# Transposes moved into freed score banks, copies ahead of norms, a split last block, and idle matmuls in TensorE's waits

## The chip, the cores and the metric

One core of a Trainium2 chip. The metric is the device time of one execution in microseconds (us), lower is better. Every run is set against runs of the kernel before on the same chip in the same rounds. A ratio is the mean time of one kernel's fast runs over the mean of the other's fast runs of the same rounds, so it is not quite the ratio of the medians that stand beside it; its interval is a 95% one.

## The reference, cut to what matters

Sliding-window attention with ALiBi, then a dense hard-swish feed-forward layer over all tokens.

```python
# q, k, v: (8 batches, 8 heads, 576, 64)
rel = pos[:, None] - pos[None, :]
mask = (rel >= 0) & (rel < 128)
scores = where(mask, q @ k.T / 8 - slope[h] * abs(rel), -1e9)
attn = softmax(scores) @ v
x = attn as (4608 tokens, 512)
h = x @ w_in                         # 512 -> 2048
out = (h * clip(h + 3, 0, 6) / 6) @ w_out    # 2048 -> 512
```

## The kernel before: the parts that matter

The kernel works in 32 steps `g`, four pairs of heads for each of eight batches. In a step TensorE makes scores in two two-bank PSUM tiles, ScalarE exponentiates them, GpSimd masks them, TensorE multiplies by v (`values`), VectorE normalises, and the result is transposed into `xT`. `fill` puts matmuls of the feed-forward layer between these parts. Batches 0 to 2 transpose q and k on TensorE (`transposes`); from batch 3 on a DMA transpose reads them out of `tbuf`, where GpSimd casts them. The pools with `PSUM` in them hold the banks that TensorE's results go to.

Names in the views: `pr` is the copy that feeds the transposes, `tp` their result, `qTb` and `kTb` the copies out of it; `scd` and `sco` are scores, `pd`, `po` and `p4buf` their exponentials, `vbuf` is v after its cast, `av` and `avh` come out of `values`, `avs` is normalised; `hps` is an up-projection, `r` and `g` what ScalarE and VectorE make of it, `ops` the down-projection. PE is TensorE, DVE VectorE, ACT ScalarE, POOL GpSimd, SP SyncE. A line of a timeline has start, length, engine, line of the kernel, operation, and in brackets how long the engine idled before and what ended that.

```python
ps_sc = tile_pool(bufs=2, space=PSUM)   # two tiles of two banks: scores
ps_h  = tile_pool(bufs=2, space=PSUM)   # two tiles of one bank: hps, tp, ...

def transposes(g):
    b, hp = divmod(g, NP)               # NP = 4
    for nm, dst in (("q", qTb[b % 2]), ("k", kTb[b % 2])):
        src = st.pop((g, nm))...
        tp = ps_h.tile([128, RT, RP], BF16, tag="h", name="tp", ...)
        for t in range(RT):             # RT = 6
            nc.tensor.transpose(tp[:, t, :], src[:, t, :], ident[:RP, :RP])
        eng = nc.scalar.copy if nm == "k" and (g == 0 or g > 2 * NP) else nc.vector.tensor_copy
        eng(out=dst..., in_=tp...)

def segment(lo, hi, fills):             # steps 5 and later
    for g in range(lo, hi + 1):
        # ... (cut)
        scores(g)
        if pe_next:
            transposes(g + 1)
        fill(f[0]); exp_diag(g, 0); fill(f[1]); exp_diag(g, 1)
        values(g - 1, (0, 1, 2))
        fill(f[2]); exp_off(g, 0); fill(f[3]); exp_off(g, 1)
        values(g - 1, (3, 4))
        # ... fill, back(g - 1), prepare(g + 2), fill, stage_next(g), fill

def stage_next(g):                      # loads, casts, DMA transposes to come
    # ... (cut)
    if g == 8:
        cast_tokens(3, "q")             # GpSimd, five casts into tbuf
    if g == 9:
        load_tokens(3, "v")
        xbar(3, "q")                    # DMA transpose out of tbuf
        cast_tokens(3, "k")             # waits for it: tbuf is one buffer
    if g == 10:
        xbar(3, "k")
    # ... (cut; batches 4 to 7 alike)
```

The softmax here doesn't subtract the row's maximum and nothing guards it: scores larger than these inputs give would overflow.

## Time and profile before

| | before |
|---|---|
| time, median of 4 fast runs | 343.48 us (342.02 to 343.56) |
| the profiled run, and its span | 340.97 us, 339.24 us |
| TensorE busy | 315.0 us, 93% |
| scores of steps 5 / 9 / 10 / 11 / 13 start | 30.6 / 58.4 / 69.2 / 79.5 / 98.1 us |
| scores of the last step start | 249.26 us |
| last matmul ends, then to the end | 334.76 us, 4.48 us |

The start of a step's scores on TensorE's timeline is the first product of q and k; in steps 0 to 8 four table matmuls start some 0.6 us ahead of it. The steps come on TensorE in the order of the program, so a change of the time shows as a shift of these starts, and the step where the shift arises holds the cause. From the start of step 13 to that of the last step all 16 traces take 149.9 to 152.1 us, so a shift that is left at step 13 reaches the end within some 2 us.

### The profile page before, as it was taken

How to read it: one execution, taken by the hardware profiler on the slowest of the kernel's cores; microseconds unless marked ns; L12 is line 12 of the kernel's file. 1: busy time of each engine (PE TensorE's matmuls, PEld its weight loads, DVE VectorE, ACT ScalarE, POOL GpSimd, SP SyncE). 2: the span in 40 equal slices, each digit the busy share in tenths (PEclk: the TensorE clock that was granted, in tenths of full speed). 3: DMA queues.
4: the chain of work that ended last, by engine and by line, in shares of the span. 5: the costliest groups of instructions: out<-in, count | busy, mean ns of one | idle time of the engine just before them, and what ended most of it. 6: DMA issues, size and time to landing. Idle time of an engine off the chain costs nothing.

```text
span 339.2 us, 6754 instructions
## 1 busy us (share of the span) xinstructions
PE 315.0 (93%) x2558; PEld 163.5 (48%) x2599; DVE 172.4 (51%) x359; ACT 200.0 (59%) x352; POOL 151.7 (45%) x261
## 2 busy tenths in 40 slices
PE   6887988899999999999999999999999999999994
PEld 5564554454444544445454544544555444444441
DVE  4576876545454554554555454555555534434400
ACT  3778666675557575767576757675765344443401
POOL 8878877717826672667356617633331000000000
PEclk9679999999999999999999999999999999999999
DMA  9999999999999999599959995310211001100021
GB/s 176 205 224 225 179 194 196 215 225 209 227 210 175 199 223 250 97 228 220 213 115 176 257 211 112 69 50 34 51 52 52 31 31 52 43 31 31 33 93 63
DMA packets 134832, 48.15 MB, mean 142 GB/s; under 512 B 121360, under 2 KB 130320, under 8 KB 134800
## 3 DMA queue, kind: packets, MB, share of 16 engines
q1 hardware_dynamic: 122464, 33.83, 54.9%
q0 software_dynamic: 8672, 7.44, 13.9%
q10 hardware_dynamic: 3664, 6.46, 5.4%
q8 instruction: 20, 0.33, 0.5%
q14 instruction: 12, 0.10, 0.1%
HBM read 36.70 MB, written 9.44 MB: 136 GB/s over the span
## 4 chain that ended last, share of the span: by engine, by line
PE 66%; ACT 9%; DVE 6%; POOL 5%; SPq 4%; DMA 4%; issue 4%; ACTq 0%; POOLq 0%
PE hps L360 29%; PE ops L377 28%; SPq L121 4%; ACT r L364 3%; DVE g L365 3%; ACT po L286 3%; DMA qTb<-tbuf 2%; DMA ldbuf<-in_k_dram 2%; POOL pd L279 2%; PE av L321 2%; PE scd L256 1%; PE av L318 1%; PE sco L262 1%; PE tp L227 1%; POOL po L289 1%
## 5 line engine op out<-in xcount | busy, mean ns | idle before, releaser
L365 DVE SCALAR_TENSOR_TENSOR g<-r,hps 128x512 bf16<-128x512 f32 x144 | 98.9, 687 | 136.0 <-ACT r L364 135.9
L364 ACT ACTIVATE r<-hps,bias 128x512 f32<-128x512 f32 x144 | 99.5, 692 | 106.3 <-PE hps L360 102.1
L360 PE MATMUL hps<-xT,w_in_sb 128*128 128x512 bf16 x546 | 144.6, 379 | 8.0 <-DVE g L365 5.5
L377 PE MATMUL ops<-w_out_sb,g 128*128 128x512 bf16 x565 | 143.5, 379 | 0.6
L377 PEld LDWEIGHTS <-g 128*128 128x128 bf16 x576 | 56.0, 98 | 65.9
L360 PEld LDWEIGHTS <-w_in_sb 128*128 128x128 bf16 x576 | 50.8, 97 | 59.5 <-issue 10.0
L289 POOL TENSOR_SCALAR_AFFINE_SELECT po<-po 128x512 bf16<-128x512 bf16 x64 | 39.9, 632 | 23.3 <-ACT po L286 20.8
L279 POOL TENSOR_SCALAR_AFFINE_SELECT pd<-pd 128x512 bf16<-128x512 bf16 x46 | 28.0, 632 | 41.2 <-ACT pd L276 41.2
L195 POOL CAST tbuf<-ldbuf 128x512 bf16<-128x512 f32 (+1 forms) x50 | 28.4, 611 | 35.3 <-issue 24.1
L286 ACT ACTIVATE po<-sco,bias_o 128x512 bf16<-128x512 f32 x64 | 43.0, 689 | 0.0
L327 DVE TENSOR_TENSOR avs<-av,rc 128x384 bf16<-128x384 f32 (+1 forms) x56 | 28.0, 500 | 1.9
L276 ACT ACTIVATE pd<-scd,bias_d 128x512 bf16<-128x512 f32 x46 | 28.9, 684 | 0.0
L321 PEld LDWEIGHTS <-pd 128*128 128x128 bf16 x256 | 18.9, 98 | 9.0 <-issue 0.4
L321 PE MATMUL av<-vbuf,pd 128*128 128x65 bf16 x240 | 22.0, 195 | 0.2 <-ACT vbuf L181 0.2
L318 PE MATMUL av<-vbuf,po 128*128 128x65 bf16 x224 | 21.6, 194 | 0.7 <-POOL po L289 0.7
L318 PEld LDWEIGHTS <-po 128*128 128x128 bf16 x256 | 19.0, 99 | 4.7 <-POOL po L289 1.0
L390 ACT COPY osb<-ops 128x512 f32<-128x512 f32 x18 | 10.5, 585 | 12.8 <-PE ops L377 12.8
L227 PE MATMUL tp<-ident,pr 96*128 96x96 bf16 x144 | 10.9, 225 | 6.7 <-DVE pr L217 2.5
L297 ACT ACTIVATE p4buf<-sco,bias_d 128x64 bf16<-128x64 f32 x46 | 14.9, 324 | 0.0
L392 DVE COPY osb<-ops 128x512 f32<-128x512 f32 x17 | 11.6, 684 | 5.8 <-PE ops L377 5.8
L217 POOL COPY pr<-ldbuf 96x768 bf16<-96x768 bf16 x17 | 13.6, 819 | 1.9 <-DMA ldbuf<-in_k_dram 1.9
L188 POOL CAST vbuf<-ldbuf 128x1024 bf16<-128x1024 f32 x14 | 14.2, 1043 | 0.0
(72 smaller groups left out, 207.6 us busy)
## 6 DMA issues: line engine op xcount, KB each, us to landing
ldbuf<-in_v_dram SPq DMA_DIRECT2D x32, 256.0 KB, 5.3
out_dram<-osb ACTq DMA_DIRECT2D x23, 256.0 KB, 3.3
ldbuf<-in_q_dram SPq DMA_DIRECT2D x20, 256.0 KB, 5.2
ldbuf<-in_k_dram SPq DMA_DIRECT2D x20, 256.0 KB, 5.7
out_dram<-osb SPq DMA_DIRECT2D x12, 256.0 KB, 2.0
w_in_sb<-in_moe_w_in_dram POOLq DMA_DIRECT2D x4, 512.0 KB, 7.4
w_out_sb<-in_moe_w_out_dram POOLq DMA_DIRECT2D x4, 512.0 KB, 10.9
ldbuf<-in_q_dram POOLq DMA_DIRECT2D x4, 288.0 KB, 7.2
```

Of the source, the lines that this page charges most:

```text
L195: nc.gpsimd.tensor_copy(out=tbuf[:m, :, j, :], in_=s[:m, j, :, :].rearrange("p (i e) d -> p i (e d)", e=2))
L276: nc.scalar.activation(out=pd[:, e, :, :].rearrange("p j c -> p (j c)"), in_=sc[:, e, :], func=ACT.Exp, bias=bias_d[:, h:h + 1], scale=scale)
L279: nc.gpsimd.affine_select(out=pd[:, e, :, :], in_=pd[:, e, :, :], pattern=[[0, 4], [1, 128]], channel_multiplier=-1, base=0, compare_op=AL ...
L286: nc.scalar.activation(out=po[:, e, :, :].rearrange("p j c -> p (j c)"), in_=sc[:, e, :], func=ACT.Exp, bias=bias_o[:, h:h + 1], scale=scale)
L289: nc.gpsimd.affine_select(out=po[:, e, :, :], in_=po[:, e, :, :], pattern=[[0, 4], [-1, 128]], channel_multiplier=1, base=-1, compare_op=A ...
L318: nc.tensor.matmul(av[:, i, e, :], lhsT=po[:, e, qt - 1, :], rhs=vb[:, qt - 1, h, :], start=True, stop=False)
L321: nc.tensor.matmul(av[:, i, e, :], lhsT=d, rhs=vb[:, qt, h, :], start=(qt == 0), stop=True)
L327: nc.vector.tensor_tensor(out=st[g, "avs"][:, qts[0]:qts[0] + nq, :, :], in0=av[:, 0:nq, :, 0:D], in1=rc[:, 0:nq, :, :].to_broadcast([128, ...
L360: nc.tensor.matmul(hps, lhsT=w_in_sb[:, ks, ts(ms, 128)], rhs=xT[:, ks, ts(nt, NT)], start=(ks == 0), stop=(ks == n_ks - 1))
L364: nc.scalar.activation(out=r6, in_=hps, func=ACT.Relu, bias=bias3[:, 0:1], scale=1.0 / 6.0)
L365: nc.vector.scalar_tensor_tensor(out=gts[nt][:, ms, :], in0=r6, scalar=1.0, in1=hps, op0=ALU.min, op1=ALU.mult)
L377: nc.tensor.matmul(ops[nt, sub], lhsT=gts[nt][:, ms, ts(sub, 128)], rhs=w_out_sb[:, ms, :], start=(ms == 0), stop=(ms == n_ms - 1))
```

## The change

It means to take the transposes of q and k for steps 6 to 11 off the two `ps_h` buffers, which the up-projections (`hps`) use too: they get one tile of the score pool, which is free once the exponentials have read it, q in its first bank and k in its second. The place of the transposes moves behind `values`. In batch 0 the copies that feed the transposes (`prepare`) go ahead of the norms, and the casts of batch 1's v are split. The last output block is split into 384 and 128 columns, so that the first part is copied while the second is computed. And unused matmuls of the identity are meant to keep TensorE's clock up.

```diff
 def transposes(g):
+    if g > NP + 1:
+        pair = ps_sc.tile([128, 2, 512], FP32, tag="sc", name="tpp")
     for nm, dst in (("q", qTb[b % 2]), ("k", kTb[b % 2])):
-        tp = ps_h.tile([128, RT, RP], BF16, tag="h", name="tp", padded_shape=[128, 8, 128])
+        if g > NP + 1:
+            tp = pair[:, "qk".index(nm), 0:S // 2].bitcast(BF16).rearrange(...)
+        else:
+            tp = ps_h.tile([128, RT, RP], BF16, tag="h", name="tp", padded_shape=[128, 8, 128])
         # six transposes into tp, then its copy, as before
 def moe_down(nt, step):
+    if nt == n_nt - 1 and sub == 3:            # the last block
+        if part == 0:
+            ops[nt] = ps_sc.tile([128, 2, 512], FP32, tag="sc", name="ops3")
+        i, lo, n = (0, 0, 384) if part < 2 else (1, 384, 128)
+        # 16 matmuls of n columns into ops[nt][:, i, 0:n], in two parts of 8
+        if part % 2:
+            nc.scalar.copy(out=osb[:, 0:n], in_=ops[nt][:, i, 0:n])
+            (nc.sync, nc.scalar)[i].dma_start(out=out[rows, lo:lo + n], in_=osb[:, 0:n])
+        return
 def first_batch():
+            spin((6, 0, 4, 0)[g])              # unused identity matmuls
+            prepare(g + 2)
+            if g == 1: spin(6)
             values(g - 1, ...)
-            prepare(g + 2)
     # step 4
-    cast_tokens(1, "v")
+    for j in range(4): cast_v(1, j, nc.gpsimd)
     exp_off(g, 0); exp_off(g, 1); transposes(g + 1); ...; prepare(g + 2)
+    cast_v(1, 4, nc.gpsimd)
 def segment(lo, hi, fills):
     scores(g)
-    if pe_next: transposes(g + 1)
     ... values(g - 1, (0, 1, 2)); fill(f[2])
+    if pe_next and g > 2 * NP: transposes(g + 1)
     exp_off(g, 0); ...; exp_off(g, 1); values(g - 1, (3, 4))
+    if pe_next and g <= 2 * NP: transposes(g + 1)
# (cut: 40 instead of 30 warm-up matmuls; two fills of steps 7 and 8 swapped;
#  step 4's second half of values in another PSUM pool)
```

More of the change, by code (lines that the diff above doesn't have):

```diff
@@ L222, in transposes @@
         b, hp = divmod(g, NP)
+        if g > NP + 1:
+            pair = ps_sc.tile([128, 2, 512], FP32, tag="sc", name="tpp")
         for nm, dst in (("q", qTb[b % 2]), ("k", kTb[b % 2])):
             src = st.pop((g, nm)).rearrange("p t e d -> p t (e d)")
-            tp = ps_h.tile([128, RT, RP], BF16, tag="h", name="tp", padded_shape=[128, 8, 128])
+            if g > NP + 1:
+                tp = pair[:, "qk".index(nm), 0:S // 2].bitcast(BF16).rearrange(
+                    "p (t a) -> p t a", t=RT)
+            else:
+                tp = ps_h.tile([128, RT, RP], BF16, tag="h", name="tp", padded_shape=[128, 8, 128])
             for t in range(RT):
@@ L308, in values @@
         if g < 2 * NP and qts[0] > 0:
-            pool, tag = (ps_h, "h") if g < NP else (ps_o, "o")
+            pool, tag = (ps_h, "h") if g < NP - 1 else (ps_o, "o")
             av = pool.tile([128, 3, 2, W], FP32, tag=tag, name="avh", padded_shape=[128, 3, 2, 85])
@@ L369, in moe_down @@
         sub, part = divmod(step, 4)
+        if nt == n_nt - 1 and sub == 3:
+            if part == 0:
+                ops[nt] = ps_sc.tile([128, 2, 512], FP32, tag="sc", name="ops3")
+            i, lo, n = (0, 0, 384) if part < 2 else (1, 384, 128)
+            for m in range(8):
+                ms = part % 2 * 8 + m
+                nc.tensor.matmul(ops[nt][:, i, 0:n], lhsT=gts[nt][:, ms, ts(sub, 128)],
+                                 rhs=w_out_sb[:, ms, lo:lo + n],
+                                 start=(ms == 0), stop=(ms == n_ms - 1))
+            if part % 2:
+                rows = ds(nt * NT + sub * 128, 128)
+                osb = rpool.tile([128, NT], FP32, tag="r6", name="osc")
+                nc.scalar.copy(out=osb[:, 0:n], in_=ops[nt][:, i, 0:n])
+                (nc.sync, nc.scalar)[i].dma_start(out=out[rows, lo:lo + n], in_=osb[:, 0:n])
+            return
         if part == 0:
@@ L381, in moe_down @@
             osb = opool.tile([128, d_model], FP32, tag="osb", name="osb")
-            if nt == n_nt - 1 and sub == 3:
-                osc = rpool.tile([128, NT], FP32, tag="r6", name="osc")
-                nc.scalar.copy(out=osb[:, 0:256], in_=ops[nt, sub][:, 0:256])
-                nc.vector.tensor_copy(out=osc[:, 0:256], in_=ops[nt, sub][:, 256:512])
-                nc.scalar.dma_start(out=out[rows, 0:256], in_=osb[:, 0:256])
-                nc.sync.dma_start(out=out[rows, 256:512], in_=osc[:, 0:256])
-                return
             if sub % 2 == 0:
@@ L471, in stage_next, with spin @@
                 cast_tokens(b + 2, "q")
+    def spin(n):
+        if n:
+            wm = ps_av.tile([128, 128], FP32, tag="av", name="wm", padded_shape=[128, 512])
+            for _ in range(n):
+                nc.tensor.matmul(wm, lhsT=ident, rhs=ident, start=True, stop=True)
     def first_batch():
@@ L487, in first_batch @@
                 scores(2)
+            prepare(g + 2)
+            if g == 1:
+                spin(6)
             if g > 0:
@@ L502, in first_batch @@
         exp_diag(g, 0)
-        cast_tokens(1, "v")
+        for j in range(4):
+            cast_v(1, j, nc.gpsimd)
         exp_off(g, 0)
@@ L514 @@
     FILLS = {5: (0, 0, 0, 0, 2, 2, 0), 6: (0, 0, 0, 0, 2, 2, 0),
-             7: (0, 0, 0, 0, 1, 2, 0), 8: (0, 0, 0, 0, 1, 2, 0)}
+             7: (0, 0, 0, 0, 2, 1, 0), 8: (0, 0, 0, 0, 2, 1, 0)}
     def segment(lo, hi, fills):
@@ L524, in segment @@
                 scores(g)
-            if pe_next:
-                transposes(g + 1)
             fill(f[0])
@@ L535, in segment @@
             fill(f[2])
+            if pe_next and g > 2 * NP:
+                transposes(g + 1)
             if g < hi:
@@ L542, in segment @@
                 values(g - 1, (3, 4))
+            if pe_next and g <= 2 * NP:
+                transposes(g + 1)
             fill(f[4])
@@ L563 @@
         wm = ps_av.tile([128, 128], FP32, tag="av", name="wm", padded_shape=[128, 512])
-        for _ in range(30):
+        for _ in range(40):
             nc.tensor.matmul(wm, lhsT=ident, rhs=ident, start=True, stop=True)
```

## The prediction

> **What bounds the kernel now.** I read the page first (busy shares, slices), then the chain of waits, then the timelines of TensorE, GpSimd and SyncE over the first 110 us, and last the tail.
>
> ```profile
> PE 315.0 (93%) x2558; PEld 163.5 (48%) x2599; DVE 172.4 (51%) x359; ACT 200.0 (59%) x352; POOL 151.7 (45%) x261
> ...
> PEclk9679999999999999999999999999999999999999
> DMA  9999999999999999599959995310211001100021
> ```
>
> TensorE is the busy engine, and from 110 us on it is the bound: busy 206.5 of the 210 us from 110 to 320 (windows view). Nothing in the change touches that stretch except its very end. So a gain must come from before 110 us or from the tail. In the first 110 us two other things stand out: the granted clock is halved in part of slices 2 to 4, and the DMA digits are 9 throughout. The two views below say which one matters.
>
> ```profile
> 95.82 1.01 SPq L121
> ...
> 97.00 7.49 DMA qTb<-tbuf
> ...
> 105.75 1.72 POOL tbuf L195 x3
> 107.47 1.17 POOL pd L279 x2
> 108.64 1.18 POOL po L289 x2
> ...
> 109.87 0.20 PE av L318
> ```
>
> This is the chain that ended last, as it crosses 95 to 110 us. TensorE's `values` of step 13 wait for the masks (affine selects) that GpSimd makes; GpSimd stood behind the cast of batch 4's k into `tbuf`; that cast needed the DMA transpose of q out of `tbuf` to land (104.49); and that transpose was issued after a row of token loads on SyncE's queue. From 81.9 to 104.5 us the chain is SyncE issues and DMA only. The same knot one batch earlier, on GpSimd's timeline:
>
> ```profile
> 62.81 1.30 POOL L195 CAST tbuf<-ldbuf 128x512 bf16<-128x512 f32 x2 [2.19 <-DMA ldbuf<-in_q_dram]
> ...
> 75.44 2.84 POOL L195 CAST tbuf<-ldbuf 128x512 bf16<-128x512 f32 x5 [7.16 <-issue]
> 78.24 1.21 POOL L279 TENSOR_SCALAR_AFFINE_SELECT pd<-pd 128x512 bf16<-128x512 bf16 x2
> 79.41 1.21 POOL L289 TENSOR_SCALAR_AFFINE_SELECT po<-po 128x512 bf16<-128x512 bf16 x2
> ...
> 104.64 2.83 POOL L195 CAST tbuf<-ldbuf 128x512 bf16<-128x512 f32 x5 [8.93 <-DMA qTb<-tbuf]
> ```
>
> GpSimd idles 7.16 us before the cast of batch 3's k: the transpose of q landed at 75.33. So the masks of step 10 come at 78.2 to 80.6 whatever TensorE does, and TensorE's `values` of step 10 started at 81.81, only 1.2 us after. And SyncE:
>
> ```profile
> 33.87 18.28 SPq L121 DMA_DIRECT2D ldbuf<-in_q_dram  x5
> 52.23 15.39 SPq L121 DMA_DIRECT2D ldbuf<-in_k_dram  x5
> 67.80 3.75 SPq L200 DMA_TRANSPOSE qTb<-tbuf  x1
> ```
>
> Its queue is solid from 33.87 on; one load of 256 KB holds it for up to 5.6 us (36.80 to 42.42). The DMA engines move 205 GB/s in the first 35 us and 192 from 35 to 60, at a busy share above 1. I read this as saturation, so the load that precedes the transpose at 67.80 cannot come sooner by much.
>
> **What the Trainium skill says.** "DMA: Bandwidth & Descriptors", section "Issuing engines are not separate DMA queues": transfers from SyncE, ScalarE and GpSimd share the same 16 engines and interleave. The trace agrees: while GpSimd's weight loads run, five q pieces of SyncE take from 33.87 to 63.44 to land; alone, five v pieces take 71.66 to 80.17. "TensorE: Matmul & The Clock Gate", Part 1: the array runs at half clock until a window of about 3.4 us was busy, and falls back after an idle one. The trace shows half clock from 7.74 to 14.56 and from 17.98 to 21.39, two pieces and one of 3.41 us. "PSUM — Partial Sum Buffer", section "Engine vs sequencer instructions": VectorE, ScalarE and GpSimd queues are strict FIFO. The trace shows it above: masks whose inputs were ready at 76 wait to 78.24 behind the cast.
>
> **The change part by part.**
>
> *Warm clock (40 instead of 30 warm-ups, 6+6+4 idle matmuls).* The warm-ups took 3.20 us for 30, 107 ns each at half clock. Ten more end at about 5.7 us at worst, where the first transpose starts anyway (5.73). They and the spins fill the windows from 4.3 to 18 us, whose matmul busy time was 1.85, 2.67, 3.26 and 1.88 of 3.4 us. If the clock holds, half-clock pieces shrink: two table matmuls 1.05 to 0.60, twelve transposes 1.14 to 0.68, eight score matmuls 0.61 to 0.49. Along batch 0's chain that is about 0.5 us at step 1 and 0.6 at step 3, some 1 us in all. The 16 spins at some 60 ns cost 1 us of waits, nothing of the path.
>
> *Copies ahead of norms, casts of v split.* The `pr` copy of step 3 ended at 17.97 on VectorE behind norms that waited for `values`; now GpSimd's copy (17.11) releases the transposes: 0.9 us. At 28.5 GpSimd waited 1.13 us for the last piece of v with masks and copies behind it; the piece now goes last. By hand, following each queue with these durations, scores of step 4 move from 24.6 to about 22.5 and the first up-projection from 28.1 to about 26.4: 2 us.
>
> *Transposes in score banks (steps 6 on).* They no longer take both `ps_h` buffers nor stand ahead of `values`. At step 5 TensorE waited for GpSimd's `pr` from 31.2 to 33.0 with `values` behind it: 1.5 us more. At steps 7 and 8 the waits for norms and products (0.84, 0.32, 1.22 us) and the 2,1 fills give about 2 us; at step 6 nothing, since the new tile waits for the first exponential (about 0.5 us). Against the kernel before, TensorE should be some 5 us early at step 9.
>
> *What of this survives.* By the views above, little. The `values` of step 10 can start no sooner than 80.6 instead of 81.81: 4 of the 5 us become an idle stretch of TensorE near 76 to 80 us. `values` of step 13 waits to about 109.9 again, less whatever the load queue gains. That gain I estimate from the one dip of the early transfers, 34 to 36 us, at 129 GB/s instead of 200: 0.35 of 2 us, 0.7 us, of which I count 0.5.
>
> *Tail.* Now: last matmul 334.77, then
>
> ```profile
> 334.79 0.37 ACT L384 COPY osb<-ops 128x256 f32<-128x256 f32 x1 [2.82 <-PE ops L377]
> 335.19 0.34 ACTq L386 DMA_DIRECT2D out_dram<-osb  x1
> 335.20 0.42 DVE L385 COPY osc<-ops 128x256 f32<-128x256 f32 x1 [6.62 <-ACT osb L384]
> 335.65 0.33 SPq L387 DMA_DIRECT2D out_dram<-osc  x1
> ```
>
> The two copies of one bank ran one after the other, 0.83 us, and the last store landed 2.3 us after its issue. New: 16 matmuls of 384 columns, then 16 of 128 in another bank, while the first part is copied and stored. 16 x 216 ns = 3.45 becomes 16 x 162 + 16 x 62 = 3.6 (an estimate from 216 ns per 512 columns and the 62 ns spacing of the five 128-column transposes): +0.15. After it one copy of 128 columns, 0.29 (as `p4buf`'s 128x128), instead of 0.83: -0.54. The half-size store on ScalarE's queue, where the other landed in 1.7, saves about 0.4. Together -0.8 us.
>
> *Sum.* -0.5 in the middle, -0.8 at the end: -1.3 us of span, from 339.2 to 337.9.
>
> From span to time: the profiled run of before took 340.97 where the timed ones took 342.02 to 343.56. If that 2.5 us is a less lucky phase of the clock windows, with TensorE late at the step 13 gate, the new kernel, which has slack ahead of it, removes it: 339.7. If it is slower transfers, both keep it: 342.2. I put slightly more on the second: **341.5 us**.
>
> **The rivals.** (1) *The early gain goes through to the end:* TensorE in order, bound from there on, everything 5 to 6 us sooner, 337 us. For it: the chain of waits before 80 us runs through the very waits removed (products, copies, norms). Against it: the 7.16 and 8.93 us idles of GpSimd, which do not depend on TensorE. It would need the transpose at 67.80 to be issued at 63. (2) *The new wait cools the clock:* idling over 3.4 us near 76 us may halve the clock for 3.4 us, 1.7 us of work. Since step 13 has only about 1 us of slack, that could eat the 0.5 and more: 343 us. For it: windows with 1.85 us busy fell cold before. (3) *Earlier weight loads crowd SyncE's loads:* GpSimd's weight loads go out 3 us sooner, and q of batch 3 lands later; but the last weight load (issued 58.15, landed 66.94) preceded the transpose already, so the bytes ahead of it are the same. No effect, or 1 us either way.
>
> **Range and chances.** 338.8 to 343.8 holds the two readings of span to time, rival 2, and half of rival 1. Faster by over 2% needs 336.6, beyond full success of rival 1: 6%. Slower by over 2% needs 350.4, and no part adds that much: 1%. Within 2%: 93%.
>
> **What would show it.** Right: step 9's scores start near 53 to 54 us instead of 58.43; the transposes out of `tbuf` still issued near 67 and 97; a wait of 3 us or more of TensorE on GpSimd's masks near 76 to 80, and a longer one at step 13; no half clock before 18 us; last matmul to end 0.8 us shorter. Wrong: the transpose issued by 64 us (then rival 1, and saturation was misread); half clock near 80 us (rival 2); scores of step 9 not early (my walk through batch 0 failed).

## The result, and the profile after

The changed kernel takes **348.06 us** (median of 4 fast runs, 347.16 to 348.99) against 343.48: ratio 1.0144, interval 1.0106 to 1.0182. It is slower by 1.4%, and outside the predicted range. Its profiled run took 347.86 us with a span of 346.12, close to its median; the profiled run of before was the lucky one (340.97), so the traces differ by 6.9 us where the medians differ by 4.6.

The page of the kernel after:

```profile
PE 316.5 (91%) x2599; PEld 166.1 (48%) x2641; DVE 172.0 (50%) x358; ACT 201.3 (58%) x353; POOL 152.9 (44%) x263
...
PE   7686876887999999999999999999999999999995
...
PEclk9899899998999999999999999999999999999999
```

TensorE does nearly the same work (316.5 us against 315.0) in a longer span. TensorE's digits stay at 6 to 8 up to slice 10, where before they reached 8 and 9 from slice 5 on, and the clock, low in slices 2 and 3 before, now dips in slices 2, 5 and 10.

| scores start, us | step 4 | 5 | 6 | 9 | 10 | 11 | 13 | last | span |
|---|---|---|---|---|---|---|---|---|---|
| before | 24.6 | 30.6 | 38.7 | 58.4 | 69.2 | 79.5 | 98.1 | 249.3 | 339.2 |
| after | 24.1 | 30.4 | 41.7 | 64.2 | 75.8 | 88.5 | 106.7 | 256.7 | 346.1 |

The kernels are level at step 5. The loss comes from step 5 to 9 (5.8 us by then) and from step 10 to 11; it then stays at 7.4 to 9. No time is lost before step 5; one wait that an edit of batch 0 brings, for the last piece of v, comes just after it (`vbuf`, 1.8 us below). The waits of TensorE from 28 to 92 us name what took the time, first before, then after (waited for, us in total, times, longest):

```profile
PE hps L360 <- DVE g L365: 3.1, 6, 1.2
PE tp L227 <- POOL pr L217: 1.4, 2, 1.0
PE tb L347 <- DVE avs L327: 1.2, 2, 0.8
PE hps L360 <- DVE qTb L229: 0.8, 2, 0.6
```

```profile
PE tpp L233 <- DVE qTb L235: 8.3, 6, 1.8
PE hps L366 <- DVE g L371: 2.0, 5, 0.5
PE avh L327 <- POOL vbuf L181: 1.8, 1, 1.8
PE tpp L233 <- ACT pd L279: 0.8, 3, 0.3
```

The waits that the change meant to remove are gone: 1.4 us for GpSimd's `pr`, 1.2 for the norms. In their place stands one that did not exist: the transposes into the new tile wait for VectorE's copy *out of it*, `qTb`, six times, 8.3 us. TensorE's timeline of the kernel after, around the first of these:

```profile
33.33 0.19 PE L327 MATMUL avh<-vbuf,p4buf 128*128 128x65 bf16 x1 [1.77 <-POOL vbuf L181]
...
33.42 0.42 PE L233 MATMUL tpp<-ident,pr 96*128 96x96 bf16 x6
34.98 0.55 PE L233 MATMUL tpp<-ident,pr 96*128 96x96 bf16 x6 [1.14 <-DVE qTb L235]
35.75 3.05 PE L366 MATMUL hps<-xT,w_in_sb 128*128 128x512 bf16 x7 [0.22 <-issue]
```

And VectorE's:

```profile
33.62 0.18 DVE L332 RECIPROCAL rc<-avh 128x4 f32<-128x4 f32 x1 [1.39 <-PE avh L327]
33.83 0.43 DVE L333 TENSOR_TENSOR avs<-avh,rc 128x256 bf16<-128x256 f32 x1
34.17 0.75 DVE L235 COPY qTb<-tpp 128x576 bf16<-128x576 bf16 x1
35.57 0.76 DVE L235 COPY kTb<-tpp 128x576 bf16<-128x576 bf16 x1 [0.64 <-PE tpp L233]
```

Read the two together. Six transposes of q go into the first bank at 33.42. VectorE copies them only after its norms, from 34.17. The six of k, which go into the *other* bank, start at 34.98, once that copy is over. Then VectorE in turn idles 0.64 us for k. Compare the kernel before at step 7, TensorE and then VectorE:

```profile
45.92 0.94 PE L227 MATMUL tp<-ident,pr 96*128 96x96 bf16 x12
```

```profile
46.38 0.76 DVE L229 COPY qTb<-tp 128x576 bf16<-128x576 bf16 x1
47.06 0.75 DVE L229 COPY kTb<-tp 128x576 bf16<-128x576 bf16 x1
```

There q and k had tiles of their own: twelve transposes in one row, and the copy of q runs beside those of k. In the built program of the kernel after, the seventh transpose of each such step carries a wait for a VectorE instruction; it waits because q and k are now two banks of one tile. In steps 9 and 10 ScalarE is drawn in as well, because there its copy of k stands ahead of half of its exponentials (`po`, `p4buf`; all engines, kernel after):

```profile
70.00 0.42 PE L233 MATMUL tpp<-ident,pr 96*128 96x96 bf16 x6 [1.85 <-DVE qTb L235]
...
70.46 0.64 ACT L235 COPY kTb<-tpp 128x576 bf16<-128x576 bf16 x1 [1.89 <-PE tpp L233]
...
71.75 1.42 POOL L295 TENSOR_SCALAR_AFFINE_SELECT po<-po 128x512 bf16<-128x512 bf16 x2 [3.34 <-ACT po L292]
```

ScalarE waits 1.89 us at the head of its queue, the exponentials behind it come late, and GpSimd's masks later still. The idle time has a second price. The windows view of the kernel after (start and end, length, busy time and instructions of each engine, granted clock, DMA share, GB/s):

```profile
31.70:35.11 3.41, 0.64 (x13) 0.53 (x13) 1.80 (x4) 1.55 (x4) 3.22 (x5) 1.00 1.24 220
35.11:38.52 3.41, 3.19 (x13) 1.42 (x13) 1.29 (x2) 0.69 (x1) 3.41 (x6) 0.50 1.21 196
...
79.48:82.89 3.41, 1.56 (x21) 0.98 (x20) 1.46 (x3) 1.49 (x3) 0.56 (x1) 1.00 1.29 178
82.89:86.30 3.41, 3.19 (x20) 1.73 (x18) 1.11 (x3) 2.10 (x5) 1.52 (x3) 0.50 1.08 226
```

After a stretch with 0.64 us of TensorE work, and again after one with 1.56, the clock is halved for 3.41 us. In the first of these stretches the wait for `vbuf` (1.77 us) is longer than the one for `qTb` (1.14). And g3_before_casts_later, which has the old transposes, is at half clock from 34.8 to 38.2 us too and takes 10.2 us for step 5, where before takes 8.1 and after 11.4: this stretch does not need the new tile. From step 5 to step 9 (30.4 to 64.2) TensorE is busy 24.72 us against 23.02 in the same steps before, at equal work: 1.7 us for the half clock. The other 4.3 of the 6.0 us by which these steps grew are idle time, where four of the six waits for `qTb` bring 4.6 us (8.3 less two of 1.85) and the one for `vbuf` 1.8, and the waits that are gone take some back.

The tail has the same wait in small. The timeline at the end of the kernel after:

```profile
341.33 0.48 ACT L388 COPY osc<-ops 128x384 f32<-128x384 f32 x1 [1.97 <-PE ops L382]
...
341.86 1.05 PE L382 MATMUL ops<-w_out_sb,g 128*128 128x128 bf16 x16 [0.57 <-ACT osc L388]
...
342.95 0.27 ACT L388 COPY osc<-ops 128x128 f32<-128x128 f32 x1 [1.14 <-PE ops L382]
343.24 0.34 ACTq L389 DMA_DIRECT2D out_dram<-osc  x1
```

The second pass, into the second bank of `ops3`, waits 0.57 us for the copy of the first. Even so the time from the last matmul to the end falls from 4.48 to 3.21 us.

### The profile page after: what moved, and what is told of

The parts are those of the page before. It is cut to its first block, busy times and chain, and to the rows that moved or that the text cites. A ratio compares the mean times of both kernels' runs of the same rounds, so it can differ in the third digit from the quotient of the medians.

```text
span 346.1 us, 6846 instructions
## 1 busy us (share of the span) xinstructions
PE 316.5 (91%) x2599; PEld 166.1 (48%) x2641; DVE 172.0 (50%) x358; ACT 201.3 (58%) x353; POOL 152.9 (44%) x263
## 4 chain that ended last, share of the span: by engine, by line
PE 72%; ACT 9%; DVE 6%; DMA 5%; POOL 4%; issue 3%; ACTq 0%; POOLq 0%
PE hps L366 32%; PE ops L398 29%; DMA ldbuf<-in_k_dram 5%; ACT r L370 4%; DVE g L371 3%; ACT po L292 3%; PE av L327 2%; PE scd L262 2%; POOL pd L285 2%; PE sco L268 2%; PE av L324 1%; ACT pd L282 1%; DVE qTb L235 1%; DVE avs L333 1%; PE sco L257 1%
## 5 line engine op out<-in xcount | busy, mean ns | idle before, releaser
L398 PE MATMUL ops<-w_out_sb,g 128*128 128x512 bf16 x549 | 140.2, 380 | 0.8 <-issue 0.2
L398 PEld LDWEIGHTS <-g 128*128 128x128 bf16 x560 | 54.5, 98 | 63.8 <-issue 0.6
L295 POOL TENSOR_SCALAR_AFFINE_SELECT po<-po 128x512 bf16<-128x512 bf16 x64 | 40.1, 636 | 33.4 <-ACT po L292 30.4
L327 PE MATMUL av<-vbuf,pd 128*128 128x65 bf16 x240 | 21.2, 194 | 0.1
L233 PEld LDWEIGHTS <-pr 96*128 96x128 bf16 x144 | 8.0, 102 | 14.5 <-issue 10.4
L303 ACT ACTIVATE p4buf<-sco,bias_d 128x64 bf16<-128x64 f32 x46 | 14.9, 324 | 0.0
L406 DVE COPY osb<-ops 128x512 f32<-128x512 f32 x17 | 11.6, 684 | 5.8 <-PE ops L398 5.8
L233 PE MATMUL tpp<-ident,pr 96*128 96x96 bf16 x72 | 5.1, 208 | 9.1 <-DVE qTb L235 8.3
```

What stands on the lines that cost most here:

```text
L295: nc.gpsimd.affine_select(out=po[:, e, :, :], in_=po[:, e, :, :], pattern=[[0, 4], [-1, 128]], channel_multiplier=1, base=-1, compare_op=A ...
L327: nc.tensor.matmul(av[:, i, e, :], lhsT=d, rhs=vb[:, qt, h, :], start=(qt == 0), stop=True)
L398: nc.tensor.matmul(ops[nt, sub], lhsT=gts[nt][:, ms, ts(sub, 128)], rhs=w_out_sb[:, ms, :], start=(ms == 0), stop=(ms == n_ms - 1))
```

## The experiments

Theory A: one tile over two banks makes k's transposes wait for the copy of q, and this is the loss. Rivals: the new place of the transposes costs by itself (B); the idle matmuls or the split casts cost (C). And a question on the prediction: is it true that an early lead cannot pass the loads and casts of batch 3 (the gate)? Five rounds each; in each row the kernel before ran in the same rounds on the same chip.

| label | median (lowest to highest), us | before, us | ratio (interval) |
|---|---|---|---|
| e1_twelve_first | 343.46 (341.49 to 346.04) | 343.22 | 1.0013 (0.9963 to 1.0062) |
| e2_old_transposes | 340.92 (339.87 to 342.06) | 343.22 | 0.9929 (0.9891 to 0.9966) |
| e3_tail_only | 341.41 (339.41 to 343.57) | 343.22 | 0.9941 (0.9898 to 0.9984) |
| e4_no_spin | 347.15 (345.19 to 348.62) | 343.22 | 1.0102 (1.0058 to 1.0147) |
| f1_two_tails | 340.21 (340.13 to 344.53) | 342.80 | 0.9953 (0.9910 to 0.9996) |
| f2_place_only | 343.54 (342.61 to 345.65) | 342.80 | 1.0034 (1.0005 to 1.0064) |
| f3_e2_no_spin | 340.39 (339.31 to 340.75) | 342.80 | 0.9927 (0.9905 to 0.9949) |
| f4_gpsimd_stores | 339.92 (339.21 to 340.75) | 342.80 | 0.9922 (0.9900 to 0.9944) |
| g1_mixed | 340.66 (338.31 to 342.51) | 342.50 | 0.9939 (0.9894 to 0.9985) |
| g2_mixed_casts_later | 336.91 (335.37 to 337.87) | 342.50 | 0.9831 (0.9791 to 0.9872) |
| g3_before_casts_later | 340.43 (339.75 to 343.18) | 342.50 | 0.9956 (0.9911 to 1.0000) |
| g4_old_v_cast | 348.40 (347.48 to 351.92) | 342.50 | 1.0173 (1.0128 to 1.0218) |
| h1_casts_and_tail | 339.06 (338.07 to 340.54) | 342.02 | 0.9916 (0.9884 to 0.9948) |
| h2_two_score_tiles | 344.72 (341.59 to 347.44) | 342.02 | 1.0047 (0.9996 to 1.0098) |

### All twelve transposes before either copy

The changed kernel; same tile, same place, only the order of issue:

```diff
     for nm, dst in (("q", ...), ("k", ...)):
         # six transposes into tp
-        eng(out=dst..., in_=tp...)
+        made.append((nm, dst, tp))
+        if g > NP + 1 and nm == "q":
+            continue
+        for n2, d2, t2 in made:        # the copies of q, then of k
+            ...
```

> The changed kernel with one thing altered: from step 6 on all twelve transposes (q and k) are issued before either copy out of the score tile. Theory A (the shared two-bank tile makes k's transposes wait for VectorE's copy of q, 8.3 us over six steps, and the idling costs clock as well): the wait of TensorE on the qT copy in front of the second six transposes is gone, steps 5 to 10 (scores of 5 to scores of 11) shrink by 8 us or more, and the time falls to 338 to 342 us, below the kernel before. Theory B (the later place of the transposes, or the score banks held until the copies are done, is what costs): the wait moves to the next scores or products and the time stays at 346 to 348. Theory C (warm-up and idle matmuls or load timing): no change, 348.

Ratio 1.0013: of the loss of 1.44%, 1.3 points are gone by this edit alone. The wait for `qTb` is absent from TensorE's list, step 9 starts at 55.7 us (before 58.4, after 64.2), and the clock is halved only once before the end, at 11.5 to 14.9 us. Theory A holds for most of the loss. But the time is no better than before, although TensorE was 2.7 us early at step 9; step 11 starts at 79.3, as before (79.5). TensorE's waits from 60 to 112 us in this run, and one of ScalarE's, tell where the lead went:

```profile
PE hps L372 <- DVE g L377: 4.5, 4, 1.8
PE tpp L234 <- ACT pd L288: 1.4, 1, 1.4
PE av L330 <- POOL po L301: 0.7, 2, 0.4
PE av L333 <- POOL pd L291: 0.7, 2, 0.4
...
ACT kTb L240 <- DVE qTb L240: 2.8, 2, 1.4
```

Two of the waits for `g` are long, 1.85 us at step 9 and 1.74 at step 10; before has none over about 0.6 us from step 9 to 11. VectorE's `g` comes late there because ScalarE's copy of k stands ahead of the exponentials and of `r`, and each time it waits 1.42 us for VectorE's copy of q, though the two read different banks. That is a second false wait: in the built program of this run ScalarE's copy waits for VectorE, in that of f2_place_only, with a buffer for each, only for TensorE. The 1.4 us for `pd` follow an output store on ScalarE's queue, at which ScalarE stood 2.5 us; in the built program this store waits for the completion semaphore of a load of batch 3's k. GpSimd waits for loads of batch 3's q too (4.74 us to 63.90), with the masks of step 9 behind, but the four waits for masks in this list all come at 109 to 111 us. So in this run the lead was not lost to the masks that the prediction named.

### The old place and the old buffers

The changed kernel with `transposes` and `segment` as before; batch 0, idle matmuls, swapped fills and split tail kept.

```diff
-    if pe_next and g > 2 * NP: transposes(g + 1)      # and the second new place
+    if pe_next: transposes(g + 1)                     # right after scores(g)
-        tp = pair[:, "qk".index(nm), ...]
+        tp = ps_h.tile([128, RT, RP], BF16, tag="h", name="tp", ...)
```

> The changed kernel with the transposes of steps 6 to 11 put back to their old place, ahead of the values, and in their old buffers; all else as changed (idle matmuls, copies ahead of norms, split casts, fills 2,1, split last block). Theories A and B: the loss is gone, 341.5 to 343.5 us, within 0.5% of the kernel before, because GpSimd and the loads hold steps 10 and 13 where they were. Theory C: still 346 to 348.

Ratio 0.9929: everything else in the change together is a gain of 0.7%, and the part "transposes in score banks" costs 2.1 points (in different rounds). The 0.8 between this run and the last one is not TensorE's false wait. I ascribe it to ScalarE's copy of k, which the new place puts ahead of exponentials at steps 9 and 10 and the shared tile keeps waiting for VectorE: the two waits of 1.85 and 1.74 us above fit, but no run isolates the place from the tile there.

### Only the split tail

The kernel before with the new last block (the `moe_down` part of the diff, nothing else).

```diff
+        if nt == n_nt - 1 and sub == 3:   # as in the change: 384, then 128 columns, tile ops3
```

> The kernel before with the split last block alone. My prediction: 0.8 us less, 342.7. Rival: in the profile of the changed kernel TensorE's last stretch is 0.76 us longer and the end after the last matmul 1.29 us shorter, so only 0.5 us less, 343.0. Either way last matmul to end falls from 4.48 to 3.2 us.

Ratio 0.9941. The trace shows 3.2 us from the last matmul to the end, as after. By the ratios that is most of the gain of the run before it. But the interval (0.2 to 1.0%) is wide, and from the start of the last step's scores to the end the trace saves only 0.5 us of 90.0, 0.15%: where the rest of the 0.6% comes from no run shows.

### Without the idle matmuls, twice

```diff
 def spin(n):
-    if n:
+    if False:
-        for _ in range(40):
+        for _ in range(30):
```

On the changed kernel:

> The changed kernel without the idle matmuls of batch 0 and with 30 warm-ups as before. If the idle matmuls are worth what I predicted (about 1 us at the start, hidden later by waits), 348 to 349. If they cost (theory C), 345 or less. The clock of 7.7 to 14.5 us should be half again.

And on the kernel with the old transposes:

> The kernel with the old transposes, without the idle matmuls and with 30 warm-ups. If the loads hold TensorE from step 10 on, as I predicted, up to 1 us at the start does not reach the end: 340.5 to 341.5. If the warm clock is worth its microsecond at the end: 342 or more. If the idle matmuls cost: under 340.

1.0102 against 1.0144 with them, and 0.9927 against 0.9929, in different rounds: no effect that the intervals resolve, so rival C falls for the idle matmuls. The first of the two still shows half clock from 32.5 and from 80.3 us, much as the kernel after does.

### The last block in two tiles

The kernel with the old transposes, with a tile for each pass:

```diff
-            if part == 0:
+            if part % 2 == 0:
                 ops[nt] = ps_sc.tile([128, 2, 512], FP32, tag="sc", name="ops3")
-                nc.tensor.matmul(ops[nt][:, i, 0:n], ...)
+                nc.tensor.matmul(ops[nt][:, 0, 0:n], ...)
```

> The kernel with the old transposes (340.92, ratio 0.9929) with the split last block in two tiles of the score pool instead of two banks of one tile. Theory A says for the tail what it says for the transposes: in one tile the second pass of matmuls waits for ScalarE's copy of the first (0.54 us between the passes in all five profiles). Then here the gap goes to under 0.1 us, last pass right after the first, time 340.4, ratio 0.9915. If the wait has another cause, the gap stays at 0.5.

The timeline at its end:

```profile
332.09 3.66 PE L377 MATMUL ops<-w_out_sb,g 128*128 128x384 bf16 x32
...
334.89 0.48 ACT L383 COPY osc<-ops 128x384 f32<-128x384 f32 x1 [1.97 <-PE ops L377]
...
335.78 0.27 ACT L383 COPY osc<-ops 128x128 f32<-128x128 f32 x1 [0.41 <-PE ops L377]
```

All 32 matmuls run in one row and the copy of the first pass lies beside them: the gap of 0.57 us is gone. So the wait goes with the tile here as well. In the time half a microsecond is too little to show against 0.4% of interval (one run of six was at 344.53).

### The new place with the old buffers

```diff
-        if g > NP + 1: tp = pair[:, "qk".index(nm), ...]
+        tp = ps_h.tile([128, RT, RP], BF16, tag="h", name="tp", ...)
```

> The changed kernel with the transposes of steps 6 to 11 at their new place, but in the two old separate buffers. Theory A (the shared tile alone costs): no wait of the second six on the copy of q, time 340.5 to 342, like the old place. If the new place is what costs beside the tile (the two copies then stand later on VectorE and ScalarE, the exponentials of steps 9 to 11 behind ScalarE's copy), 343 to 345, like the kernel with twelve transposes first (343.46).

Ratio 1.0034, 1.1 points better than the changed kernel. But its profiled run (345.65, the slowest of the six) starts step 9 at 64.4, as late as the changed kernel; it is earlier only from step 10 on. TensorE then waits for `qTb` 3.8 us and for `kTb` on ScalarE 1.6, now with the *up-projections* that want the `ps_h` buffers back, because the copies stand behind VectorE's norms. So the new place isn't free either (rival B holds in part): behind `values`, the copies queue behind norms.

### A score tile of its own for k

The cleanest separation of A: place and order as in the change, one line more.

```diff
+            if NP + 1 < g <= 2 * NP + 1 and nm == "k":
+                pair = ps_sc.tile([128, 2, 512], FP32, tag="sc", name="tpk")
```

> The changed kernel with one edit: for the transposes of steps 6 to 9, k gets a score tile of its own (q's copy still issued ahead of k's transposes, same place; steps 10 and 11 keep the shared tile). Theory of the shared tile: of the six waits for VectorE's copy of q (8.3 us) the two late ones of 1.85 us stay and the four early ones go, scores of step 9 start at 56 to 59 instead of 64.2, time 344 to 346. Rival, that the order of issue on TensorE makes the wait whatever the tile: step 9 at 63 to 65, the waits stay, time 347 to 349.

TensorE's waits from 28 to 92 us in this run:

```profile
PE tpp L235 <- DVE qTb L237: 3.7, 2, 1.8
PE tpk L235 <- ACT p4buf L302: 2.7, 3, 0.9
PE hps L368 <- DVE g L373: 2.4, 6, 0.5
PE avh L329 <- POOL vbuf L181: 1.7, 1, 1.7
```

The four early waits for the copy of q are gone and the two late ones, whose tile I left shared, are there: 3.7 us, 2 times. That settles the wait: with order and place unchanged, it goes with the shared tile. The ratio, 1.0047, is 1 point better than the changed kernel's (median 344.72; one of the six, 347.44, is slow, and the five fast ones have 344.18). But step 9 started at 64.1 in the profiled run, not at 56 to 59: that expectation missed. Two things took the place of the waits. The second score tile is free only after the last exponential (2.7 us for `p4buf`), and the wait for v's last piece fell in a window (from 32.30 us) with only 1.10 us of work, after which the clock was halved again. The profiled run was the slowest of the five fast ones (346.71). So what the wait costs in time rests on e1_twelve_first; here and in f2_place_only the wait is gone, and steps 5 to 9 of the profiled run are nearly as slow as in the changed kernel (32.8 and 33.1 us against 33.9).

### The casts of v as before

```diff
-        for j in range(4):
-            cast_v(1, j, nc.gpsimd)
+        cast_tokens(1, "v")
-        cast_v(1, 4, nc.gpsimd)
```

> The changed kernel with the casts of batch 1's v as before: three casts in one block, the last piece not moved behind the copies. Theory that the late last piece costs: the wait of values on it (1.8 us at step 4) goes, scores of step 6 start 1 us or more before 41.7, the half clock at 35 us may go, time 346 to 347. Rival, that the false wait of the shared tile swallows it: step 6 at 41.5 to 42, time 347.5 to 348.5, as the changed kernel. If the split was the gain that I predicted (2 us by step 4), it is slower: step 5 starts after 31.5, 349 or more.

Ratio 1.0173 against 1.0144, overlapping. The wait of `values` on the last piece of v is gone, and a wait on GpSimd's masks of 3.2 us, which now stand behind the whole cast, takes its place. So the moved piece is not what made the change slow, and it is not the harmless step that I called it either: either way GpSimd is late here.

### Output stores issued from GpSimd

With the old transposes TensorE still lost time at step 12: scores 12 to 13 took 11.6 us. ScalarE's timeline of e2_old_transposes:

```profile
91.61 0.69 ACT L365 ACTIVATE r<-hps,bias 128x512 f32<-128x512 f32 x1 [3.78 <-DMA ldbuf<-in_q_dram]
```

In the built program the store of the output that stands ahead of this line on ScalarE's queue waits for a completion semaphore that it shares with a load of q, and ScalarE waits with it.

```diff
-            eng = nc.sync if done[0] == G else nc.scalar
+            eng = nc.sync if done[0] == G else nc.gpsimd
```

> As the two-tile version, with the output stores issued from GpSimd instead of ScalarE until the last step. In the profile of the kernel with the old transposes ScalarE stood 3.78 us behind a store that waited for a load of q (their completion shares a semaphore), and TensorE waited 2.1 us at step 12. If that is a link by which the loads hold TensorE, steps 12 to 13 (scores) shrink from 11.7 to under 10 us and the time falls by 1 to 2 us, to 338.5 to 339.5. If GpSimd's masks hold it anyway, step 13 or 14 gives it back and the time stays at 340.4; if the stores queue behind GpSimd's waits, it is slower.

(On top of f1_two_tails.) Step 12 then takes 9.1 us and step 10 takes 13.8, where TensorE waits 2.4 us for GpSimd's `pr`. But its base, f1_two_tails, has the same without this edit (9.1 and 14.5 us, 2.8 us for `pr`), so the edit is not shown to move anything; the stall falls at step 12 in e2_old_transposes and at step 10 in f1, f3 and f4. The time is 0.9922 against 0.9953, with overlapping intervals.

### The best parts together, and the gate lifted

g1_mixed: the changed kernel with all twelve transposes first for steps 6 to 9, old place and buffers for steps 10 and 11, the tail in two tiles.

```diff
-        if g > NP + 1:
+        if NP + 1 < g <= 2 * NP + 1:     # tile of the score pool; q and k issued before the copies
+            if pe_next and g > 2 * NP: transposes(g + 1)   # right after scores(g), as before
```

> The best parts together: the twelve transposes of steps 6 to 9 in the shared score tile at the new place, all issued before either copy; those of steps 10 and 11 at the old place in the old buffers; the last block in two tiles. Theory that the loads and GpSimd's casts gate steps 9 to 11: the scores of step 9 start near 55.7 us as in e1_twelve_first, but the transposes out of tbuf still go out at 66.5 to 68.5 and 96 to 97.5, the lead is gone by step 11 (79 to 81 us), and the time is 339.5 to 341, no better than e2_old_transposes. Rival, that only the false waits kept the early gain from arriving: step 11 starts by 77.5 and the time is 337 to 338.5.

g2_mixed_casts_later: the same, with GpSimd's casts of batch 3's q and k (and k of later batches) one step later, right ahead of the DMA transpose that reads them.

```diff
-        if g == 8:
-            cast_tokens(3, "q")
         if g == 9:
             load_tokens(3, "v")
+            cast_tokens(3, "q")
             xbar(3, "q")
-            cast_tokens(3, "k")
         if g == 10:
+            cast_tokens(3, "k")
             xbar(3, "k")
```

> g1_mixed with GpSimd's casts of batch 3's q and k (and of later batches' k) one step later, right ahead of the DMA transpose that reads them, so that the masks of steps 9 and 10 no longer stand behind casts that wait for loads. Gate theory: GpSimd's idle of 7 to 9 us ahead of the masks goes, scores of step 10 start by 64.5 and of step 11 by 75, and if TensorE is the bound from there the time is 337.5 to 339. Rival, that the data of batch 3 itself (needed at step 12 for scores) come no sooner than before: step 12 starts at 88 to 91 as in the others, the wait only moves there, and the time stays 339.5 to 342.

Two controls: the kernel before with these later casts, and that one with the two-tile tail besides.

> The kernel before with the same later casts and nothing else: a control. Gate theory: the kernel before had 1 us of slack or less at steps 10 and 13, so it gains at most 1 us, 342 to 343.5 against 343. Rival: if later casts by themselves give 2 us or more (below 341), then what g2_mixed_casts_later shows isn't owed to the early lead. If they delay the DMA transposes, slower: 344 or more.

> The kernel before with the later casts of batch 3's and later q and k and the last block in two tiles; no new place or tile for the transposes, no idle matmuls, no split casts of v. Theory that the early lead is worth something once the gate is lifted: this control has no lead, so it stays at 338.3 to 340 (343 less 2 for the casts less 1.5 to 2 for the tail), 1.5 us or more above g2_mixed_casts_later at 336.9. Rival, that the casts and the tail are all of it: 336.5 to 337.7.

GpSimd's timeline in g1_mixed with a line of TensorE's, and then GpSimd's in g2_mixed_casts_later:

```profile
64.59 0.62 POOL L195 CAST tbuf<-ldbuf 128x512 bf16<-128x512 f32 x1 [5.71 <-DMA ldbuf<-in_q_dram]
...
67.10 1.21 POOL L291 TENSOR_SCALAR_AFFINE_SELECT pd<-pd 128x512 bf16<-128x512 bf16 x2
...
69.69 1.58 POOL L217 COPY pr<-ldbuf 96x768 bf16<-96x768 bf16 x2
70.56 0.43 PE L234 MATMUL tp<-ident,pr 96*128 96x96 bf16 x6 [2.58 <-POOL pr L217]
...
75.19 2.85 POOL L195 CAST tbuf<-ldbuf 128x512 bf16<-128x512 f32 x5 [3.92 <-issue]
77.99 1.22 POOL L291 TENSOR_SCALAR_AFFINE_SELECT pd<-pd 128x512 bf16<-128x512 bf16 x2
```

```profile
61.06 1.21 POOL L291 TENSOR_SCALAR_AFFINE_SELECT pd<-pd 128x512 bf16<-128x512 bf16 x2 [5.11 <-ACT pd L288]
...
66.23 2.85 POOL L195 CAST tbuf<-ldbuf 128x512 bf16<-128x512 f32 x5
71.40 1.22 POOL L291 TENSOR_SCALAR_AFFINE_SELECT pd<-pd 128x512 bf16<-128x512 bf16 x2 [2.33 <-ACT pd L288]
```

The masks of step 9 come at 61.06 instead of 67.10 and those of step 10 at 71.40 instead of 77.99; they now wait for the exponentials, that is, for TensorE, and no longer stand behind a cast. The step starts:

| scores start, us | step 9 | 10 | 11 | 13 | last | span |
|---|---|---|---|---|---|---|
| g1_mixed | 56.6 | 67.4 | 82.0 | 100.3 | 250.2 | 338.9 |
| g2_mixed_casts_later | 56.4 | 67.2 | 77.5 | 95.8 | 245.7 | 334.4 |
| h1_casts_and_tail | 59.1 | 69.9 | 80.2 | 98.4 | 248.5 | 337.2 |

With the lead and the gate (g1_mixed) step 11 starts at 82.0, later than in the kernel before: TensorE waits 2.58 us at step 10, not for the masks themselves but for `pr`, which GpSimd copies behind them and behind the casts that wait for loads; and the clock is halved from 72.2 to 75.6 us. In g2 this wait is gone. The time is 340.66. With the lead and no gate step 13 starts at 95.8, 2.4 us before the kernel before, and the time is **336.91 us, 1.7% below the kernel before, and better than both kernels**. My number for step 10 (64.5) missed: step 9 takes the same 10.7 us. The later casts alone (g3_before_casts_later) gave 0.9956, 2 us by the medians and at the edge of the interval. That is the number that I had set for the rival, that the casts are all of it and the lead nothing, so it had to be tested with the tail besides: h1_casts_and_tail gives 0.9916. The lead is then worth 0.85 points (0.9916 less 0.9831), some 2.9 us of 342.5, in different rounds; the two intervals do not overlap. The traces agree: against h1 the steps of g2 start 2.7 us earlier at step 9, 2.7 at step 13 and 2.8 at the last one. (The lead holds the parts of batch 0 too: at step 5 it is 0.6 us.)

## Why the prediction was wrong, point by point

**The failed step is "Transposes in score banks".** It counted the waits that the move removes, some 5 us ahead by step 9, and allowed for one new wait, on the first exponential, of 0.5 us. That one exists (0.8 us, three times together). What it left out is that q and k share one tile over two banks: k's transposes wait for VectorE's copy of q. I had the sizes of the copies and VectorE's strict order before me and did not ask who must have *left* the tile before its second half is written. Where I counted 1.5 and 2 us of gain, the trace has 8.3 us of new waits over six steps, and two stretches of 3.41 us at half clock, the first behind a wait for `vbuf` as well. Step 9 was at 64.2 us instead of 53 to 54. The check that I set for it ("scores of step 9 not early: my walk failed") is the one that fired, though I had tied it to batch 0. With the order turned so that the wait is gone (e1_twelve_first), the gain was 2.7 us at step 9, half of my 5; in the profiled runs of f2 and h2, with the wait gone by other buffers and the place kept, there was none.

**Rival 2, "the new wait cools the clock", came true at another wait.** Half clock stood at 35.1 and 82.9 us. I looked for it behind the masks near 76 to 80 us; in the kernel after it came behind the false waits and the one for `vbuf`, 1.7 us over steps 5 to 9. In g1_mixed, where TensorE has no false wait but the gate, it came where I had looked, a little sooner (72.2 us).

**"What of this survives: little" was right in outcome, and in part by another path.** In e1_twelve_first and g1_mixed a lead of 1.8 to 2.7 us at step 9 was gone by step 11. In g1 it was GpSimd behind the loads, as I said, and moving the casts let it through; but TensorE waited 2.58 us for `pr` up to 70.6 us, and no run shows the wait of 3 us or more on masks near 76 to 80. In e1 ScalarE took it. The DMA transpose out of `tbuf` was issued at 68.3 us in the kernel after and at 66.7 to 68.4 in e1, e2 and g1, near the 67 that I set (the second one, in the kernel after, at 100.5 instead of 97, behind the late steps). Rival 1, 337 us, falls for the change as written; it is what came when the gate was lifted, by an edit that the change does not have.

**The clock and the idle matmuls:** the mechanism held only in part. The kernel after still had half clock before 18 us (11.2 to 14.6); of the ten profiled kernels with these matmuls three (f1, g1, g4) had none before 30 us, of the six without them not one was spared (3.1 us of half clock before 30 us on average against 6.8, one trace of each). But taking them out changed the time of neither kernel. The saving of some 1 us was not there.

**Copies ahead of norms, split casts:** twelve of the profiled kernels have the copies ahead of the norms. Seven of them start step 4 at 22.2 to 23.0 us (predicted 22.5), and five, the kernel after among them, at 24.1 to 25.3; the four without start it at 24.6 to 25.1. In the kernel after the load for step 1 landed late (its copy on VectorE starts at 9.05 us, in e1 at 7.76); why the other four are late, no run isolates, nor has any run this part alone. So the 2 us came in most runs, but not in the measured trace. "The piece now goes last" was no saving: `values` waits for it up to 2.3 us (g1_mixed; 1.8 in the kernel after).

**The tail:** the sum was about right, the terms were not. After the last matmul 1.27 us were saved (4.48 to 3.21), where I had counted 0.94; but the matmuls cost 0.57 us more for the second shared tile, beside about 0.2 for the smaller columns (I had 0.15). Net 0.5 instead of 0.8.

**A reading:** the half clock before lies at 7.74 to 21.39 us, in slices 1 to 3 of the page, not 2 to 4 as I wrote. Nothing rests on it.

Range and chances followed: I gave slower by more than a few tenths hardly a chance because no *listed* part could add time. The list lacked the part.

## What to carry to other kernels

When two independent results are put into one PSUM tile, check in the built program whether the second producer waits for the first consumer, or one consumer for the other, even if they lie in different banks; issuing both producers before either consumer takes away the first wait, a tile for each takes away both. Before moving work ahead, find the gate that does not depend on it, and move what stands in front of the gate: here GpSimd's casts, one step later, let a lead through that did not show in the time without that. And count the waits that a new buffer *brings* as carefully as those that it takes away.

## What the Trainium skill lacked or had wrong

- "PSUM — Partial Sum Buffer", section "PSUM bank collisions raise a hardware error": its rule is to guard by bank and quadrant. It says nothing of guards that are wider than that, which the building of the program can set. Here a tile over two banks serialised its banks: 8.3 us over six waits between a write to one bank and a read of the other, and 0.57 us in the tail; in e1_twelve_first also two reads, ScalarE's of one bank behind VectorE's of the other, 2.8 us over two waits. With a tile for each, the four waits changed and the tail's one were gone.
- "TensorE: Matmul & The Clock Gate", Part 1: the half clock is told as following an idle window, and frequent short idling is told to bring it too, but without a figure of how little work does it. Here partly busy windows of 3.41 us were followed by it: 1.87 and 1.82 us busy (before), 2.06 (e2_old_transposes), 1.56 (after). Others stayed at full clock after 1.93 (after, from 41.93 us) and even 1.62 (h2_two_score_tiles, from 66.43 us). The busy time in the records alone does not decide it, and no run here shows what does.
- No page that I found tells that a store on one engine's queue can wait for a completion semaphore that loads on another queue hold: ScalarE stood still for 3.78 us in e2_old_transposes, and the step took 11.6 us, in f1_two_tails 9.1.
